# Probabilities times v: twelve rounded products on the whole array, or six float32 products on its halves

## The chip, the cores and the metric

The kernel runs on one core of a Trainium2 chip, in one launch. The core has a matrix engine (TensorE, PE in the profile; its weight loads are PEld), three engines for elementwise work (VectorE or DVE, ScalarE or ACT, GpSimd or POOL) and a queue that issues transfers (SyncE, SP). The metric is the device time of one execution in microseconds, lower is better; it is the median of several runs.

## The reference

Three layers follow one another. The first is attention for 2 batches, 8 heads, 768 positions and a head dimension of 64, in which a query sees only the keys of its own cluster:

```python
q_assign = np.argmax(np.einsum('bhsd,hcd->bhsc', q_n, c_n), axis=-1)
k_assign = np.argmax(np.einsum('bhsd,hcd->bhsc', k_n, c_n), axis=-1)
mask = q_assign[:, :, :, None] == k_assign[:, :, None, :]
scores = np.where(mask, scale * np.matmul(q, k.transpose(0, 1, 3, 2)), -1000000000.0)
attn = np.exp(scores - np.max(scores, axis=-1, keepdims=True))
attn = attn / (np.sum(attn, axis=-1, keepdims=True) + 1e-09)
out = np.matmul(attn, v)
```

The second layer takes these 1536 rows of 512 through `h = x @ w_in` (1024 wide), a softmax gate, a layer norm with gain and `@ w_out`. The third is `(x @ w_a) * (x @ w_b) @ w_out`, 1536 wide. All is float32; the weights come as 64-bit floats and are turned into float32 on the chip.

## The kernel before

**Two number formats.** Most products are made in a rounded float32 format (`F32R`, "fp32r" in the profile) in which TensorE streams one column per cycle. To keep float32's accuracy an operand is split into its rounded value (hi) and what is left (lo), and a product becomes two or three products. A plain float32 product needs no split; TensorE makes it in two passes, and each shows as an instruction of its own in the trace.

**Attention.** Sixteen heads lie in 8 pairs `n`. A step is one tile of 128 queries of one head; there are 96. Per step `score` makes four products into one of two PSUM areas (`psS0`, `psS1`), DVE takes the row maximum (L1017), ACT the exponential with the row sum (L1021). `turn` transposes the 128 x 768 probabilities in two halves of three tiles (L1045) into `psT0` and `psT1`; ACT copies each half out rounded (L1062, hi) and DVE subtracts it from PSUM (L477, lo). Two steps make a group of 256 queries, 48 in all. `apply` multiplies a group by v, in two parts (`part` 0 and 1) of three key tiles each: per key tile the stationary operand holds v's hi and lo side by side (128 columns), and hi and lo of the probabilities stream over it (L1077), six products a part, twelve a group, all into the one bank `psO`. Its lower and upper 64 rows are then added: ACT copies both halves (L1092, L1097) and POOL adds them (L1098). A last step multiplies by the inverse row sums (L1116 to L1127) and splits the result for the next layer. `do_v` makes v's hi and lo on POOL (L482, L824).

**Preparation.** q and k of the next pair are transposed, split, compared with the centroids and laid out by transfers between the steps of the present pair (L740, L838, L842, L921 on TensorE).

**The later layers.** `moe_h` (L1187), `moe_lnt` (L1260) and `moe_x2` (L1277) are the second layer; `moe2_ab` (L1330) and `moe2_y` (L1358) the third. Their weights are loaded and split by `weight` (L570 to L602) in two staging areas (`RU`).

**Order.** Nothing is issued where it is written. Every operation is added to a plan with an engine, an estimated cost, a rank and the cells of memory that it reads and writes. The planner simulates the engines with these costs, takes at each engine's free moment the ready operation with the lowest rank, and so fixes each engine's order. Ranks come from the step's number, from small tables (`SUB`, `LEAD`, `P0`, `P1`) and from a long table of corrections (`ADJ`). On the chip the engines keep that order and wait by semaphores.

**Warm-up.** `FILL` = 26 products of the identity matrix (L704 to L711) go to TensorE at the start with a rank behind all else, wherever it would have nothing to do. In the kernel before they are of four kinds: 12 transposes, 2 float32 products on the whole array (L706), 2 of 64 columns (L708), and 10 float32 products with 64 stationary columns that take the left and the right half of the array in turn (L711, `tile_position`).

Of the kernel before, what the change touches and what calls it, by code (L numbers as in the profile page):

```python
# [26 lines left out]
LO = {'lna': (12, (2, 3, 4, 5, 9, 10, 11)), 'qk0': (4, (2, 3)), 'turn': (24, ()), 'arg': (8, (2, 3, 4, 5, 6, 7)), 'w': (8, (0, 1, 2, 3, 4, 5, 6, 7)), 'xlo': (3, (0, 2)), 'vhi': (2, (0, 1)), 'rb': (3, (1, 2)), 'xhi': (3, (0, 1, 2)), 'merge': (6, (0, 1, 2, 3, 4, 5)), 'nmul': (3, (0,)), 'qk': (4, (0, 2, 3)), 'wc': (8, (0, 1, 2, 4, 5, 6, 7))}  # L27
FILL = 26

P0 = {'q': 0.676, 'a': 0.526, 's': -1.817, 'do_v': -4.684, 'do_sim0': 1.842, 'do_arg': 0.4, 'do_oh0': 7.789}  # L30
P1 = {'a': -6.508, 's': 0.229, 'do_place': 16.159, 'do_v': -8.279, 'do_sims': 3.084, 'do_arg': -13.543, 'do_oh': -1.51, 'do_ohd': -29.092, 'qk_part': -21.079}
ADJ = {
# [35 lines left out]
    "do_oh 7.0 PE": -28.061, "do_oh 7.1 ACT": -3.7, "do_oh 7.1 PE": 4.601, "do_oh ACT": -42.439,  # L68
# [157 lines left out]
    "turn ACT": -0.037, "turn DVE": -19.442,  # L226
}
BR = {'h': 3.102, 'ln': 2.949, 'lnt': 7.533, 'x2': 11.917, 'dm': 0.03, 'ts': 2.583}


class Plan:

# [158 lines left out]
def tile_cluster_attention_moe_moe2(  # L391
# [22 lines left out]
    P = 128  # L414
# [215 lines left out]
    def hlo(n):  # L630
        return X0 + 2 * 3072 if n in (1, 3) else HL_
# [810 lines left out]
```

## Time and profile before

| | |
|---|---|
| median of 3 runs | 741.63 us (741.13 to 741.98) |
| profiled execution, its own time | 741.5 us |
| its span, first to last instruction | 739.4 us |
| busy: PE, PEld | 710.1 us (96%), 620.4 us (84%) |
| busy: DVE, ACT, POOL | 455.7, 398.8, 327.7 us |
| mean granted TensorE clock | 0.986 of full |

Busy time of PE is the union of its instructions' durations, and a duration holds some 0.16 us of pipeline that overlaps the next instruction; what an instruction keeps TensorE for is therefore read from one start to the next. 2.1 us of the execution lie outside the span.

### The profile page before, as it was taken

The page shows a single profiled execution, that of the slowest core. Times are in us where ns is not written, and L with a number is a line of the kernel's source. Part 1 is how long each engine was busy: PE and PEld are TensorE (multiplying, and loading weights), DVE is VectorE, ACT ScalarE, POOL GpSimd, SP SyncE. Part 2 cuts the span into 40 slices and gives each one's busy share as a digit, 9 for nine tenths or more (in the row PEclk, how much of TensorE's full clock was granted, in tenths as well). Part 3 has the DMA queues.
Part 4 walks back from the last instruction along what each step waited for, and adds up shares of the span by engine and source line. Part 5 has one row for each costly group of instructions (what it writes and reads, how often), then busy time and mean ns, then how long its engine had stood idle before and what let it go on. Part 6 is the DMA issues. An engine that isn't in the chain of part 4 may idle for free.

```text
span 739.4 us, 11619 instructions
## 1 busy us (share of the span) xinstructions
PE 710.1 (96%) x4166; PEld 620.4 (84%) x4166; DVE 455.7 (62%) x832; ACT 398.8 (54%) x849; POOL 327.7 (44%) x405
## 2 busy tenths in 40 slices
PE   7979899899989999999999999999999999999997
PEld 5778789799879988878999989888888888888886
DVE  5867988889868988999995716863221432111123
ACT  5768789899969998566435523443122321121111
POOL 5135986668766743666542727772130600000000
PEclk9999999999989999999999999999999999999999
DMA  4266745455363410232220313332020100010011
GB/s 154 62 141 163 177 106 132 93 145 138 84 152 72 104 59 1 86 103 97 86 87 29 107 37 114 115 120 80 1 86 0 41 18 1 1 57 1 1 57 58
DMA packets 39098, 58.53 MB, mean 79 GB/s; under 512 B 3832, under 2 KB 33920, under 8 KB 39040
## 3 DMA queue, kind: packets, MB, share of 16 engines
q1 hardware_dynamic: 39040, 57.79, 27.8%
q8 instruction: 33, 0.54, 0.3%
q14 instruction: 25, 0.20, 0.1%
HBM read 36.74 MB, written 3.15 MB: 54 GB/s over the span
## 4 chain that ended last, share of the span: by engine, by line
PE 66%; DVE 10%; ACT 9%; DMA 7%; issue 4%; POOL 3%; SPq 0%; DVEq 0%; ACTq 0%; POOLq 0%
PE psS L1358 13%; PE psT L1330 13%; PE psO L1330 7%; PE psM L1330 7%; PE psS L1187 5%; DMA F<-in_moe_w_in_dram 4%; PE psO L1277 4%; PE psM L1277 3%; PE psO L1077 3%; PE psS L1013 3%; DVE R L477 3%; PE psT L1045 3%; DVE mxn L1017 3%; ACT R L1062 3%; ACT F L1021 3%
## 5 line engine op out<-in xcount | busy, mean ns | idle before, releaser
L477 DVE TENSOR_TENSOR R<-psT,R 128x384 fp32r<-128x384 f32 (+1 forms) x216 | 118.9, 565 | 29.4 <-ACT R L1062 24.4
L475 POOL TENSOR_TENSOR R<-F,R 128x512 fp32r<-128x512 f32 (+1 forms) x76 | 87.9, 1159 | 93.2 <-ACT R L601 72.4
L1344 DVE TENSOR_TENSOR R<-F,R 128x512 fp32r<-128x512 f32 x36 | 27.6, 768 | 151.5 <-ACT R L1343 151.5
L1330 PE MATMUL psT<-R 128*128 128x512 f32 x432 | 103.8, 390 | 0.2 <-ACT F L1341 0.2
L1358 PE MATMUL psS<-R 128*128 128x512 f32 x432 | 100.5, 389 | 0.0
L1045 PE MATMUL psT<-ident,F 128*128 128x128 f32 x576 | 92.1, 278 | 7.5 <-DVE R L477 6.5
L1062 ACT CAST R<-psT 128x384 fp32r<-128x384 f32 x192 | 89.6, 482 | 15.6 <-PE psT L1045 13.1
L1013 PE MATMUL psS<-R 128*128 128x512 f32 (+3 forms) x384 | 94.7, 370 | 1.0 <-ACT F L1021 0.8
L1330 PEld LDWEIGHTS psT<-R 128*128 128x128 f32 x432 | 80.8, 188 | 17.7 <-ACT F L1341 1.1
L1358 PEld LDWEIGHTS psS<-R 128*128 128x128 f32 x432 | 81.1, 188 | 16.8
L1343 ACT CAST R<-F 128x512 fp32r<-128x512 f32 x36 | 22.4, 622 | 133.5 <-PE psS L1358 132.7
L1077 PE MATMUL psO<-R 128*128 128x256 f32 x576 | 92.1, 296 | 1.9 <-ACT F L1097 1.8
L1017 DVE TENSOR_REDUCE mxn<-psS 128x1 f32<-128x768 f32 x96 | 90.7, 946 | 4.4 <-PE psS L1013 4.3
L1021 ACT ACTIVATE F<-psS,mxn 128x768 f32<-128x768 f32 x96 | 87.4, 910 | 3.3 <-DVE mxn L1017 2.9
L592 POOL TENSOR_TENSOR F<-F 128x512 int32<-128x512 int32 x45 | 61.3, 1362 | 45.7 <-DVE F L588 33.9
L1077 PEld LDWEIGHTS psO<-R 128*128 128x128 f32 x576 | 75.6, 191 | 4.4 <-ACT F L1097 3.5
L1045 PEld LDWEIGHTS psT<-ident,F 128*128 128x128 f32 x576 | 66.9, 142 | 13.8 <-DVE R L477 9.0
L1013 PEld LDWEIGHTS psS<-R 128*128 128x128 f32 (+1 forms) x384 | 68.5, 198 | 11.1 <-ACT F L1021 1.7
L1187 PE MATMUL psS<-R 128*128 128x512 f32 x288 | 69.2, 394 | 2.0 <-DVE F L1208 2.0
L570 ACT ACTIVATE F<-F 128x512 f32<-128x512 f32 x48 | 32.5, 678 | 67.8 <-DMA F<-in_moe_w_a_dram 22.3
L1187 PEld LDWEIGHTS psS<-R 128*128 128x128 f32 x288 | 52.9, 188 | 12.8 <-DVE F L1208 2.5
L1330 PE MATMUL psO<-R 128*128 128x512 f32 x216 | 51.9, 389 | 0.0
(157 smaller groups left out, 1076.8 us busy)
## 6 DMA issues: line engine op xcount, KB each, us to landing
F<-in_moe_w_out_dram SPq DMA_DIRECT2D x20, 512.0 KB, 3.2
R<-R SPq DMA_DIRECT2D x28, 288.0 KB, 5.1
F<-in_moe_w_b_dram SPq DMA_DIRECT2D x12, 512.0 KB, 3.5
F<-in_moe_w_a_dram SPq DMA_DIRECT2D x12, 512.0 KB, 3.5
R<-R SPq DMA_DIRECT2D x28, 192.0 KB, 5.3
F<-in_moe_w_in_dram SPq DMA_DIRECT2D x8, 512.0 KB, 6.0
F<-in_v_dram SPq DMA_DIRECT2D x8, 384.0 KB, 3.8
out_dram<-F SPq DMA_DIRECT2D x12, 256.0 KB, 2.1
```

Of the source, the lines that this page charges most:

```text
L475: pl.add("POOL", pool(n), rank, lambda: G.tensor_tensor(out=out_, in0=in0, in1=in1, op=ALU.subtract), reads, writes)
L477: pl.add("DVE", dve(n), rank, lambda: V.tensor_tensor(out=out_, in0=in0, in1=in1, op=ALU.subtract), reads, writes, port=port)
L592: pl.add("POOL", pool(n), rank, lambda: G.tensor_tensor(out=u, in0=u, in1=low, op=ALU.add), [rk, lwk], [uk])
L1013: T.matmul(sp[:, c0:c0 + cn], kq[:r, 2 * m, t * P:(t + 1) * P], kq[:r, 2 * m + 1, c0:c0 + cn], start=m == 0, stop=m == 1)
L1017: pl.add("DVE", dve(S), i + SUB["max"], lambda: V.tensor_reduce(out=mxn[:, b:b + 1], in_=sp[:, :S], axis=AX.X, op=ALU.max, negate=True), [ ...
L1021: pl.add("ACT", act(S) + 93 + 93, i + SUB["exp"], lambda: A.activation(F[:, po:po + 768], sp[:, :S], AF.Exp, bias=mxn[:, b:b + 1], scale=1 ...
L1045: T.transpose(sp[:, c, :], pt[:, kt * P:(kt + 1) * P], ident)
L1062: pl.add("ACT", act(HN), rk, lambda sp=sp, dh=dh: A.copy(dh, sp), [sk], [hk])
L1077: T.matmul(psO[:, :GN], vs[:, kt, j].rearrange("p l d -> p (l d)"), pt[:, m, kt, :], start=(kt == 0 and m == 0), stop=(kt == NT - 1 and m ...
L1187: T.matmul(sp[:, n0:n0 + 512], xv5[:, i, a, c], winv[:, w, c, n0:n0 + 512], start=first, stop=(c == KD - 1 and a == 1))
L1330: T.matmul(pt, w[:, l, c, :], xv5[:, xs, a, c, :], start=first, stop=(c == KD - 1 and l == 1))
L1358: T.matmul(yv[t][0], hl2[a][:, ts_], wo[:, l, :], start=(first and a == 0 and l == 0), stop=(last and a == 1))
```

## The change

A group's probabilities stay plain float32, as they come out of the transposes, and v stays as it was loaded. `apply` makes one float32 product per key tile, with the 64 columns of v as the stationary operand on one half of the array, even key tiles on the left half and odd ones on the right. A part is thus three products: left, right, left in part 0 and right, left, right in part 1. The two halves of `psO` are added as before, now by ACT (a copy) and DVE (an addition that reads PSUM). `turn` has one copy per half: `psT0` by DVE, `psT1` by ACT. `do_v` is gone, and v is loaded into one of two places of its own. All 26 warm-up products are transposes. The memory that this frees holds a fourth set of q/k operands and a second pair of split buffers (`KQS`, `HLS`), and the last layer's weight loads have four staging areas for two; three of that layer's weight pieces are loaded early for six, and 25 of them have a place for 28. The planner counts `PVC` for a part. `ADJ` has other numbers throughout, `P0` and `P1` are shorter.

```diff
+PVC = 3 * 216.0 + 15.0
+TDM, TD = 4, (0, 2)
...
-    RU = ((5376, 6400), (6912, 7936))
+    KQS, HLS = (20480, 23552, 26624, 36608), (30464, 33536)
+    VS = (1536, 6016)
+    RU = ((5376, 6400), (6912, 7936), (8448, 9472), (9984, 11008))
...
         for x in range(FILL):
-            if x < 12:
-                fn, cost = lambda: T.transpose(psO[:, :P], ident, ident), 107
-            elif x < 14:
-                fn, cost = lambda: T.matmul(psO[:, :256], ident, wide, start=True, stop=True), 107
...
+            pl.add("PE", 107, 1e6 + x, lambda: T.transpose(psO[:, :P], ident, ident), ["ident"], ["psO"])
...
-            pl.add("ACT", act(HN), rk, lambda sp=sp, dh=dh: A.copy(dh, sp), [sk], [hk])
-            sub("turn", i * 2 + hf, HN, rk, dl, sp, dh.bitcast(F32), [sk, hk], [lk])
+            if (2 * i + hf) % TDM in TD:
+                pl.add("DVE", dve(HN), rk, lambda sp=sp, dh=dh: V.tensor_copy(dh, sp), [sk], [hk])
+            else:
+                pl.add("ACT", act(HN), rk, lambda sp=sp, dh=dh: A.copy(dh, sp), [sk], [hk])
...
-                for kt in range(part * HT, (part + 1) * HT):
-                    for m in range(2):
-                        T.matmul(psO[:, :GN], vs[:, kt, j].rearrange("p l d -> p (l d)"), pt[:, m, kt, :],
-                                 start=(kt == 0 and m == 0), stop=(kt == NT - 1 and m == 1))
...
-            pl.add("PE", mm_cost(GN, 6), i + SUB["pv"] + 1 + part, mm, [rc(*rd)], ["psO"], after=70.0)
+                for kt in ks:
+                    rs = slice(kt % 2 * D, (kt % 2 + 1) * D)
+                    T.matmul(psO[rs, :GN], vs[:, j, kt % HT * 2 + kt // HT], pt[:, kt, :], start=kt < 2, stop=kt >= NT - 2,
+                             tile_position=(0, kt % 2 * D), skip_group_check=True)
...
+            pl.add("PE", PVC, i + SUB["pv"] + 1 + part, mm, [fc(*rd)], ["psO"], after=70.0)
...
-            if on_pool("merge", n * 6 + j * 3 + g):
...
-                pl.add("ACT", act(GN) + 110, rk, lambda: A.copy(tv[hi], psO[hi, :GN]), ["psO"], [tk])
-                pl.add("POOL", pool(GN), rk, lambda: G.tensor_tensor(
-                    out=xv[hi], in0=tv[hi], in1=xv[hi], op=ALU.add), [tk], [hk])
+            pl.add("DVE", dve(GN), rk, lambda: V.tensor_tensor(
+                out=xv[hi], in0=psO[hi, :GN], in1=xv[hi], op=ALU.add), ["psO"], [hk])
```

TensorE's order in the middle of the attention, before: the transposes (L1045), the scores (L1013) and, six products at a time, the parts of `apply` (L1077).

```order
L1045 MATMUL psT_67<-ident,F 128x128 x3
L1077 MATMUL psO<-R 128x256 x6
L1045 MATMUL psT_68<-ident,F 128x128 x3
L1077 MATMUL psO<-R 128x256 x6
L1045 MATMUL psT_67<-ident,F 128x128 x3
L1013 MATMUL psS_66<-R 128x512 x2
L1013 MATMUL psS_66<-R 128x256 x2
```

The same place after (L1021 transposes, L989 scores, L1047 `apply`).

```order
L1021 MATMUL psT_68<-ident,F 128x128 x3
L1047 MATMUL psO<-F 64x256 x3
L1021 MATMUL psT_67<-ident,F 128x128 x3
L989 MATMUL psS_65<-R 128x512 x2
L989 MATMUL psS_65<-R 128x256 x2
L1021 MATMUL psT_68<-ident,F 128x128 x3
L1047 MATMUL psO<-F 64x256 x3
L989 MATMUL psS_66<-R 128x512 x2
```

A part is three products for six, on 64 stationary columns, and work for the whole array stands on either side of it. Of the 96 parts 94 stand alone like this, and two stand together as six.

DVE's order there, before: two subtractions (L477) and one maximum (L1017) per step.

```order
L477 TENSOR_TENSOR R<-psT_68,R 128x3x128
L1017 TENSOR_REDUCE mxn<-psS_66 128x1
L477 TENSOR_TENSOR R<-psT_67,R 128x3x128
L1017 TENSOR_REDUCE mxn<-psS_65 128x1
L477 TENSOR_TENSOR R<-psT_68,R 128x3x128
```

After (L1028 the copy of `psT0`, L1062 the addition of the halves of `psO`, L993 the maximum).

```order
L1028 COPY F<-psT_67 128x3x128
L1062 TENSOR_TENSOR F<-psO,F 64x256
L993 TENSOR_REDUCE mxn<-psS_65 128x1
L1067 TENSOR_SCALAR rinv<-rsum 128x4
L1028 COPY F<-psT_67 128x3x128
L993 TENSOR_REDUCE mxn<-psS_66 128x1
```

One copy per step stands where there were two subtractions, and the addition is new here.

TensorE at the start, before: the warm-up products ahead of the first comparison with the centroids (L799).

```order
L774 MATMUL psT_68<-ident,F 64x128 x3
L704 MATMUL psO<-ident 128x128
L706 MATMUL psO<-ident 128x256 x2
L708 MATMUL psO<-ident 128x64 x2
L711 MATMUL psO<-ident 64x256 x10
L799 MATMUL psT_67<-cb,R 128x64 x6
```

After (L763 is L774, L702 the warm-up, L788 is L799).

```order
L763 MATMUL psT_67<-ident,F 64x128 x3
L700 MATMUL psM<-ident,F 128x128
L763 MATMUL psT_68<-ident,F 64x128 x3
L702 MATMUL psO<-ident 128x128 x13
L788 MATMUL psM<-cb,R 128x64 x6
```

Thirteen transposes stand where there were one transpose and fourteen products.

## Rows read from the trace of the kernel before

**Rows 1.** Windows: busy us (instructions) by engine, granted clock, DMA share, GB/s.
```profile
19.00:303.00 284.00, 266.09 (x1869) 241.80 (x1869) 239.44 (x437) 242.55 (x575) 176.31 (x240) 0.97 0.43 107
...
150.00:200.00 50.00, 49.14 (x368) 45.55 (x368) 45.97 (x85) 48.71 (x119) 35.66 (x49) 1.00 0.44 121
...
350.00:400.00 50.00, 50.00 (x339) 46.22 (x338) 41.81 (x96) 21.95 (x40) 19.55 (x21) 1.00 0.20 64
...
500.00:550.00 50.00, 50.00 (x223) 41.40 (x222) 13.83 (x21) 14.10 (x24) 13.72 (x13) 1.00 0.17 55
```

**Rows 2.** Timeline of PE near the attention's end: start us, us, engine line op.
```profile
285.57 0.96 PE L1013 MATMUL psS<-R 128*128 128x512 f32 x4
286.36 0.88 PE L1077 MATMUL psO<-R 128*128 128x256 f32 x6
287.08 0.82 PE L1045 MATMUL psT<-ident,F 128*128 128x128 f32 x6
287.65 3.01 PE L1187 MATMUL psS<-R 128*128 128x512 f32 x12
290.51 0.82 PE L1045 MATMUL psT<-ident,F 128*128 128x128 f32 x6
```

**Rows 3.** Groups of PE by form, 19 to 303 us: count | busy us, mean ns | idle before.
```profile
L740 PE MATMUL psM<-ident,F 128*128 128x128 f32 x81 | 15.3, 302 | 0.0
L838 PE MATMUL psM<-R,cb 128*128 128x384 f32 x56 | 13.0, 353 | 0.1
L1187 PE MATMUL psS<-R 128*128 128x512 f32 x48 | 11.8, 395 | 0.0
L1116 PE MATMUL psM<-ident,F 128*128 128x128 f32 x46 | 9.0, 276 | 0.5 <-ACT F L747 0.4
L921 PE MATMUL psM<-ident,F 128*128 128x128 f32 x42 | 7.9, 300 | 6.7 <-POOL F L893 3.5 <-ACT R L924 3.1
L842 PE MATMUL psM<-ident,F 128*128 128x128 f32 x42 | 7.3, 281 | 0.1
```

**Rows 4.** Timeline of PE in the warm-up.
```profile
7.33 0.56 PE L708 MATMUL psO<-ident 128*128 128x64 f32 x4
7.82 2.38 PE L711 MATMUL psO<-ident 128*64 128x256 f32 x20
10.12 0.41 PE L799 MATMUL psT<-cb,R 128*128 128x64 f32 x2
```

**Rows 5.** Windows of L711 alone: PE busy (instructions under way), PEld, clock, DMA.
```profile
7.80:7.83 0.03, 0.01 (x2) 0.02 (x2) 1.00 1.35 512
7.83:8.05 0.22, 0.22 (x2) 0.18 (x4) 1.00 1.01 377
8.05:8.10 0.05, 0.05 (x4) 0.02 (x2) 1.00 1.14 430
```

**Rows 6.** Chain of waits, 6.5 to 11 us: start us, us, what.
```profile
6.63 0.87 PE psO L706 x4
...
10.19 0.79 PE psT L799 x6
```

**Rows 7.** Waits of PE's weight loads, 19 to 303 us: total, times, longest.
```profile
PEld psT L1045 <- DVE R L477: 9.0, 18, 3.0
PEld psM L921 <- POOL F L893: 3.9, 2, 3.7
...
PEld psO L1077 <- ACT F L1097: 3.5, 8, 1.2
```

**Rows 8.** Groups of DVE, ACT and POOL by line, 19 to 303 us.
```profile
L477 DVE TENSOR_TENSOR R<-psT,R 128x384 fp32r<-128x384 f32 x192 | 102.7, 550 | 25.8 <-ACT R L1062 24.4
L1127 DVE TENSOR_TENSOR F<-F,psM 128x256 f32<-128x256 f32 x15 | 6.1, 408 | 0.2 <-PE psM L1116 0.2
L1062 ACT CAST R<-psT 128x384 fp32r<-128x384 f32 x192 | 89.6, 482 | 15.6 <-PE psT L1045 13.1
L1097 ACT COPY F<-psO 64x256 f32<-64x256 f32 x47 | 17.2, 367 | 0.6
```

More of the change, by code (lines that the diff above doesn't have):

```diff
@@ L441, in tile_cluster_attention_moe_moe2 @@
     ps = ctx.enter_context(tc.tile_pool(name="ps", bufs=1, space=PSUM))
[L444 to L447 removed]
+    X0, WIN_, OHT_ = 0, 12288, 29696
+    KQS, HLS = (20480, 23552, 26624, 36608), (30464, 33536)
+    WO_, EW_, LNT_, HLC_ = 20480, 28672, 31744, 12288 + 6144
+    R = const.tile([P, 39936], F32R, name="R")
+    NAT_, P_, SIM_, OHP_, XS_, RB_, PT_ = 0, 2304, 3840, 4224, 4992, 5760, 8448
+    VS = (1536, 6016)
     E_, LN_, WG_, ACC_, BS_ = 0, 2048, 4096, 0, 4096
[L449 to L452 removed]
+    RU = ((5376, 6400), (6912, 7936), (8448, 9472), (9984, 11008))
+    OUT_, CT_ = 5376, 11520
+    F = const.tile([P, 11904], F32, name="F")
     psS = [ps.tile([P, 1024], F32, name=f"psS{i}") for i in range(2)]
@@ L609, in tile_cluster_attention_moe_moe2 @@
     NPR = len(pairs)
-    nat = [F[:, NAT_ + 768 * i:NAT_ + 768 * (i + 1)].rearrange("p (h t d) -> p h t d", h=2, t=NT) for i in range(3)]
+    nat = [F[:, NAT_ + 768 * i:NAT_ + 768 * (i + 1)].rearrange("p (h t d) -> p h t d", h=2, t=NT) for i in range(2)]
     nat1 = [F[:, RU[1][0] + 768 * i:RU[1][0] + 768 * (i + 1)].rearrange("p (h t d) -> p h t d", h=2, t=NT) for i in range(2)]
@@ L630, in hlo @@
     def hlo(n):
-        return X0 + 2 * 3072 if n in (1, 3) else HL_
+        return HLS[n % 2]
     def hlv(n):
@@ L700, in centroids @@
         pl.add("PE", 213, Rk, lambda: T.transpose(psM[:, :P], F[:, CT_ + 128:CT_ + 256], ident), [cd, "ident"], ["psM"])
-        wide = ident.unsqueeze(1).to_broadcast([P, 2, P])
         for x in range(FILL):
-            if x < 12:
-                fn, cost = lambda: T.transpose(psO[:, :P], ident, ident), 107
-            elif x < 14:
-                fn, cost = lambda: T.matmul(psO[:, :256], ident, wide, start=True, stop=True), 107
-            elif x < 16:
-                fn, cost = lambda: T.matmul(psO[:, :D], ident, ident[:, :D], start=True, stop=True), 107
-            else:
-                rs = slice(x % 2 * D, (x % 2 + 1) * D)
-                fn, cost = lambda rs=rs: T.matmul(psO[rs, :256], ident[:, :D], wide, start=True, stop=True,
-                                                  tile_position=(0, rs.start), skip_group_check=True), 107
-            pl.add("PE", cost, 1e6 + x, fn, ["ident"], ["psO"])
+            pl.add("PE", 107, 1e6 + x, lambda: T.transpose(psO[:, :P], ident, ident), ["ident"], ["psO"])
         cpv = psM[:, :P].rearrange("p (a h c) -> p a h c", a=NHP, h=2)
@@ L816, in do_place @@
             dma((0, 96 * (d1 - d0)) if rows else (96 * (d1 - d0), 0), rk, lambda dst=dst, src=src: Y.dma_start(dst.bitcast(F32), src.bitcast(F32)), rd, wr)
-    def do_v(n, j, rk):
-        vs = vsv(n).rearrange("p (r a) j l d -> p r a j l d", r=2)
-        vh, vl = vs[:, :, :, j, j, :], vs[:, :, :, j, 1 - j, :]
-        src = nat[2][:, j].rearrange("p (a r) d -> p r a d", r=2)
-        ck = rc(*[(vso(n) + t * 256 + j * 128, 128) for t in range(NT)])
-        copy("vhi", n * 2 + j, 384, rk, vh, src, [natk(n, 2)], [ck])
-        pl.add("POOL", pool(384), rk, lambda: G.tensor_tensor(
-            out=vl, in0=src, in1=vh.bitcast(F32), op=ALU.subtract), [natk(n, 2)], [ck])
     def do_sims(n, s, rk, bk):
@@ L1045, in tr @@
                     T.transpose(sp[:, c, :], pt[:, kt * P:(kt + 1) * P], ident)
-            dh = dst[:, 0, hf * HT:(hf + 1) * HT, tt * P:(tt + 1) * P]
-            dl = dst[:, 1, hf * HT:(hf + 1) * HT, tt * P:(tt + 1) * P]
-            hk, lk = (rc(*[(o + m * 1536 + kt * 256 + tt * P, P) for kt in range(hf * HT, (hf + 1) * HT)]) for m in range(2))
+            dh = dst[:, hf * HT:(hf + 1) * HT, tt * P:(tt + 1) * P]
+            hk = fc(*[(o + kt * 256 + tt * P, P) for kt in range(hf * HT, (hf + 1) * HT)])
             rk = i + SUB["t1" if hf else "t0"]
             pl.add("PE", 330, rk, tr, [pk], [sk])
-            if on_pool("turn", i * 2 + hf):
-                so = OHT_ + 768 + hf * HN
-                st = R[:, so:so + HN].bitcast(F32).rearrange("p (c n) -> p c n", c=HT)
-                tk = rc((so, HN))
-                pl.add("ACT", act(HN), rk, lambda sp=sp, st=st: A.copy(st, sp), [sk], [tk])
-                pl.add("POOL", 150 + 0.86 * HN, rk, lambda st=st, dh=dh: G.tensor_scalar(
-                    out=dh, in0=st, scalar1=1.0, scalar2=0.0, op0=ALU.mult, op1=ALU.add), [tk], [hk])
-                pl.add("POOL", pool(HN), rk, lambda st=st, dh=dh, dl=dl: G.tensor_tensor(
-                    out=dl, in0=st, in1=dh.bitcast(F32), op=ALU.subtract), [tk, hk], [lk])
-                continue
-            pl.add("ACT", act(HN), rk, lambda sp=sp, dh=dh: A.copy(dh, sp), [sk], [hk])
-            sub("turn", i * 2 + hf, HN, rk, dl, sp, dh.bitcast(F32), [sk, hk], [lk])
+            if (2 * i + hf) % TDM in TD:
+                pl.add("DVE", dve(HN), rk, lambda sp=sp, dh=dh: V.tensor_copy(dh, sp), [sk], [hk])
+            else:
+                pl.add("ACT", act(HN), rk, lambda sp=sp, dh=dh: A.copy(dh, sp), [sk], [hk])
     def apply(i, part):
@@ L1092, in apply @@
             pl.add("ACT", act(GN) + 110, rk, lambda: A.copy(xv[hi], psO[lo, :GN]), ["psO"], [hk])
-            if on_pool("merge", n * 6 + j * 3 + g):
-                to = XT_ + g % 2 * 256
-                tv = F[:, to:to + 256]
-                tk = fc((to, 256), rows=1 << j)
-                pl.add("ACT", act(GN) + 110, rk, lambda: A.copy(tv[hi], psO[hi, :GN]), ["psO"], [tk])
-                pl.add("POOL", pool(GN), rk, lambda: G.tensor_tensor(
-                    out=xv[hi], in0=tv[hi], in1=xv[hi], op=ALU.add), [tk], [hk])
-            else:
-                pl.add("DVE", dve(GN), rk, lambda: V.tensor_tensor(
-                    out=xv[hi], in0=psO[hi, :GN], in1=xv[hi], op=ALU.add), ["psO"], [hk])
+            pl.add("DVE", dve(GN), rk, lambda: V.tensor_tensor(
+                out=xv[hi], in0=psO[hi, :GN], in1=xv[hi], op=ALU.add), ["psO"], [hk])
             return
@@ L1118, in apply @@
         pl.add("PE", 2 * 107, rk, tr, [rbk], ["psM"])
-        if on_pool("nmul", n * 3 + g):
-            to = XN_ + g % 2 * 256
-            tv = F[:, to:to + 256]
-            tk = fc((to, 256))
-            pl.add("ACT", act(GN), rk, lambda: A.copy(tv, psM[:, :GN]), ["psM"], [tk])
-            pl.add("POOL", pool(GN), rk, lambda: G.tensor_tensor(
-                out=xv, in0=xv, in1=tv, op=ALU.mult), [tk], [xk])
-        else:
-            pl.add("DVE", dve(GN), rk, lambda: V.tensor_tensor(
-                out=xv, in0=xv, in1=psM[:, :GN], op=ALU.mult), ["psM"], [xk])
+        pl.add("DVE", dve(GN), rk, lambda: V.tensor_tensor(
+            out=xv, in0=xv, in1=psM[:, :GN], op=ALU.mult), ["psM"], [xk])
         ts = range(b * NT + g * GT, b * NT + (g + 1) * GT)
@@ L1292, in tile_cluster_attention_moe_moe2 @@
     US = 3.27
-    PIECES = [EW_ + i * 1024 for i in range(6)] + [WIN_ + i * 1024 for i in range(6)]
+    PIECES = [EW_ + i * 1024 for i in range(3)] + [WIN_ + i * 1024 for i in range(6)]
     PIECES += [LNT_ + i * 1024 for i in range(8)] + [WO_ + i * 1024 for i in range(8)]
@@ L1311, in load_w2 @@
         o = piece(f, x)
-        weight(rank, src, shp, o, o + 512, RU[(f * 3 + x) % 2], "ACT", f * 3 + x)
+        weight(rank, src, shp, o, o + 512, RU[(f * 3 + x) % 4], "ACT", f * 3 + x)
     outv = out.rearrange("(b p a r) d -> b r a p d", b=B, a=HT, r=2)
```

201 lines of the change are left out of this document (92 added, 109 removed), and 232 rows, old and new, of the table ADJ.

## The prediction

> **What bounds the kernel now.** I read the windows first. From 350 us to the end TensorE is busy all the time (50.00 of 50 us) while the others fall to a third of that [rows 1]: the two later layers are bound by TensorE, the change leaves their products as they are, and what the attention gains or loses arrives at the end undiminished. The attention, 19 to 303 us, is different: PE 266, ACT 243, DVE 239 of 284 us, and in its best stretch (150 to 200 us) PE 49.1 and ACT 48.7 of 50 [rows 1]. Three engines are near their limit, and PE first.
>
> A busy PE is no measure, so I counted what the work keeps TensorE for, start to start. In the timeline the four score products of a step take 285.57 to 286.36 = 0.79 us, one part of `apply` 0.72, the six transposes 0.57: 2.08 per step, 200 us for 96 steps [rows 2]. The groups by form add 211 transposes (81 + 46 + 42 + 42) at 0.11 (the six with the tail that the next product's start hides), 23 us, and 56 products of 384 columns at 0.18 (by columns from the 0.12 of a product of 256), 10 us, and 48 of the second layer at 2.86 / 12, 11 us [rows 2, 3]; some 2 us are small. That is **246 us of work in 284**, so 38 us are lost: 17.9 visibly idle (284.0 - 266.1), about 8 by the clock (0.97 granted on the mean, 284 x 0.03), the rest in gaps that lie under the pipeline's overlap [rows 1]. The waits of the weight loads name the causes: 9.0 us for DVE's subtraction that frees `psT`, 3.5 for ACT's second copy that frees `psO`, and 3.9 for the cluster masks of the next pair [rows 7].
>
> **What leaves ACT, DVE and POOL.** DVE loses 192 subtractions of 0.550 and gets 96 copies of 384 elements from PSUM; the trace has no such copy in bulk, so between 0.482 (ACT's copy of the same tile) and 0.550, and I take 0.55. It also gets 48 additions at about 0.41 (the like one of L1127): 103 - 53 - 20 = 30 us less, 209 of 284. ACT loses 96 copies of 0.482 and 48 of 0.367, 64 us, and stands at 179 [rows 8]. POOL loses the additions and v's split. None of these three can bound the attention any more, and the waits for `psT`'s subtraction and for the second copy of `psO` have nothing left to wait for but one copy or one addition.
>
> **What the new product costs TensorE.** This is the term that decides, and the warm-up of before happens to contain it: L711 is the float32 product with 64 stationary and 256 streamed columns, left and right half in turn. Ten products are 20 instructions, two passes each [rows 4]. Two weight loads start at once and two more some 0.05 later, two passes start together, and the next two only after 8.05 [rows 5]; ten pairs lie between 7.82 and 10.12 [rows 4]. A whole-array float32 product has two passes of 0.87 / 4 = 0.217 [rows 6], and ten times that is 2.17. So a pass on a half takes as long as one on the whole array; what the halves save is that a left and a right pass run side by side.
>
> In the warm-up that is ten products in ten slots. A part of `apply` is **three** products, left, right, left, and work for the whole array stands on both sides. The left half has two products, four passes, one after another; the right half's two passes run beside the first two and it is then empty. That is four slots, 4 x 0.217 = 0.87 us, not three. To it comes the way into the half mode and out of it: L711 keeps TensorE 2.30 where its slots make 2.17, so 0.13 more (the first weight load, which nothing hides, and the wait before L799), and L708's four passes take 0.49, where four passes of 64 columns made one after another for L799 take 4 x 0.79 / 6 = 0.53 [rows 4, 6] or, by their columns, 0.22; the entry thus costs between nothing and 0.27, and I take 0.10. **A lone part costs 0.87 + 0.23 = 1.10 us, where six rounded products cost 0.72: 0.38 more.** Its bounds: 0.15 more if entry and exit are hidden, 0.55 more with the dear entry, and 0.07 less if three products took three slots (0.65) and the switches nothing. 94 lone parts at 0.38 and the one pair (six slots and one switch, 1.53 against 1.44) make **+36 us of TensorE's work**, 282 in place of 246.
>
> The Trainium skill (TensorEngine Tiling, Theoretical Speedup) has an array split in two for 64 columns or fewer at up to twice the speed. By it a part would be 3 x 0.435 / 2 = 0.65 and the change would save TensorE 7 us. The trace bears that out for an even, unbroken alternation only.
>
> **What of the 38 lost us goes.** With 282 us of work TensorE is the one bound, and the pace of a step stays near the old 2.96 us (284 / 96) while DVE has an eighth and ACT a quarter less to do. I take away the waits for `psT` and `psO` (9.0 + 3.5, and 1.5 of like ones), 4 of the 6.7 us before the masks' transposes, since POOL has less in its queue [rows 3, 7], and 5 of the 8 at the slow clock, since fewer long waits let it fall: 23. That leaves 15, between 0 and the whole 38. Those who wait behind DVE's new copy and addition are its maximum (L1017 before) and through it the exponential; with DVE at 209 of 284 I cost that at nothing, and it would cost part of the 38 if the cover were gone.
>
> **The rest.** The warm-up before L799 shrinks from 7.33 to 10.12 to transposes of 0.11, thirteen in all: at most 1.4 us earlier, and I take 1. v's loads go straight to their place, one transfer per pair as before, so SP's queue has the same number. The fourth set of q/k operands lets the placing transfers start earlier; nothing waits for them in the weight loads' list. The last layer has fewer weight pieces early and more staging areas; TensorE does not wait from 350 us on [rows 1], the three other engines that split the weights have spare time there, and if that cover were too thin a piece's load and split would show as a gap of some us. All that at nothing, ± 2.
>
> **The sum**, against the profiled execution's 741.5 (0.1 below the median of 741.63): + 36 - 23 - 1 = + 12, **753.5, forecast 753**.
>
> **The rivals.**
> *The switches hide (faster).* The next weights are loaded during the lone left passes, and the last whole-array product drains beside the first half products; or the second passes pair better and a part takes three slots plus the switches (0.65 + 0.23). Then a part costs 0.87 to 0.88, 0.15 more, 14 us; - 23 - 1 makes **731**. For it: weight loads run ahead of products all through the trace. Against it: the one stretch of half products in the trace holds TensorE 0.13 longer than its slots [rows 4, 6], and in it nothing of L799 ran ahead. With neither extra slot nor switch it would be 720. The point from which it decides: a part under 0.97 us (24 / 95 + 0.72). Chance 0.20.
> The skill (TensorEngine Tiling, Key Properties) says that a change of tiling mode drains TensorE; this speaks against hidden switches, it names no price, and the two switches of rows 4 agree with it.
> *TensorE fills completely.* All 38 us go: + 36 - 38 - 1 = **738 to 742**, no change. For it: from 350 us on it does run without a gap. Against it: the first head's chain, in which nothing else is ready, and the masks' transposes wait for other engines' results and not for a free one. Chance 0.08.
> *The waits stay (slower still).* Other orders, one `psO` whose addition now stands in DVE's queue, and a clock that falls more often because a lone half counts for little: nothing of the 38 goes, 741.5 + 36 - 1 = **776**. For it: the granted clock is 0.97 on the attention's mean already [rows 1]. Against it: rows 7 names waits that the change removes. Chance 0.10.
> *The forecast*, 743 to 764: chance 0.62.
>
> **How the numbers follow.** What can be told from no change is 0.2%, 1.5 us. Faster: 0.20 of the first rival, 0.04 of the second (its 738 to 740) and 0.03 of the forecast's lower tail, 0.27. Same: the rest of the second and 0.01 of that tail, 0.05. Slower: 0.58 of the forecast and 0.10 of the third, 0.68. The range takes in the first rival's middle and most of the third: 729 to 774; the forecast's own is 743 to 764.
>
> **What would show it.** In the profile after, a part of `apply` keeps TensorE 1.10 us to the next operation's start, and its six passes start as two pairs and then two alone; if it is under 0.97, the first rival holds. PE's busy time in the attention is over 96%, ACT and DVE stand at some 60 and 70%, and the attention ends about 12 us later. From 350 us on nothing may differ but the shift. I am wrong if a part costs 1.1 and the end is still not later: then the 38 us were worth more than I gave back.

## The result, and the profile after

The changed kernel takes **751.48 us** (median of 4 runs, 750.52 to 752.12) where the kernel before took 741.69 in the same comparison (741.13 to 741.98): a ratio of 1.0132, 95% interval 1.0114 to 1.0149. It is slower by 9.8 us; 12 had been forecast. The profiled executions have spans of 739.4 and 750.3 us.

The windows of the changed kernel, in the columns and stretches of [rows 1]:

```profile
19.00:303.00 284.00, 279.02 (x1793) 201.26 (x1792) 206.48 (x375) 186.10 (x413) 112.28 (x150) 0.99 0.42 106
150.00:200.00 50.00, 50.00 (x329) 35.84 (x327) 35.62 (x66) 34.33 (x77) 20.98 (x28) 1.00 0.40 101
350.00:400.00 50.00, 49.32 (x334) 45.44 (x332) 45.46 (x101) 23.44 (x43) 28.05 (x28) 1.00 0.28 91
500.00:550.00 50.00, 50.00 (x223) 41.40 (x222) 13.19 (x18) 12.76 (x23) 8.83 (x10) 1.00 0.13 43
```

In the attention TensorE is busy for 279 of 284 us (266 before), DVE for 206 (239), ACT for 186 (243), POOL for 112 (176). Three engines were near their limit; now one is, and it shows no idle time between 150 and 200 us.

TensorE's timeline near the attention's end, which answers to [rows 2]:

```profile
284.64 1.08 PE L1047 MATMUL psO<-F 128*64 128x256 f32 x6
285.65 0.88 PE L1021 MATMUL psT<-ident,F 128*128 128x128 f32 x6
286.28 0.96 PE L989 MATMUL psS<-R 128*128 128x512 f32 x4
287.17 1.08 PE L1047 MATMUL psO<-F 128*64 128x256 f32 x6
```

From start to start, a part of `apply` keeps TensorE 1.01 us (0.72 before), the six transposes behind it 0.63 (0.57), and the four scores ahead of it, whose end holds the change into the half mode, 0.89 (0.79). A step is 2.53 us where it was 2.08: 0.45 more, though the part has half as many products.

Most parts stand behind transposes and not behind scores. The first two rows are such a part after, the last two one before:

```profile
115.64 0.82 PE L1021 MATMUL psT<-ident,F 128*128 128x128 f32 x6
116.39 1.08 PE L1047 MATMUL psO<-F 128*64 128x256 f32 x6
```
```profile
284.52 0.96 PE L1077 MATMUL psO<-R 128*128 128x256 f32 x6
285.32 0.49 PE L1045 MATMUL psT<-ident,F 128*128 128x128 f32 x3
```

Six transposes ahead of a part keep TensorE 0.75 us (0.57 elsewhere), so the way into the half mode takes 0.18 there. But a rounded part behind transposes kept it 0.80 and not 0.72, so the change again costs 0.45: 0.18 ahead, 0.21 in the part (1.01 for 0.80) and 0.06 behind.

The windows of L1047 alone over one part (PE busy with the instructions under way, PEld, clock, DMA) answer to [rows 5]:

```profile
201.48:201.70 0.22, 0.21 (x2) 0.20 (x4) 1.00 0.32 105
201.70:201.75 0.05, 0.05 (x2) 0.00 (x0) 1.00 0.09 31
201.75:201.96 0.21, 0.21 (x4) 0.14 (x1) 1.00 0.16 37
201.96:202.18 0.22, 0.22 (x3) 0.14 (x1) 1.00 0.12 35
202.18:202.49 0.31, 0.31 (x2) 0.00 (x0) 1.00 0.09 30
```

Two passes start in the first window, two in the third, and one each in the fourth and the fifth (the counts hold passes that are still ending): two pairs and then two alone, four slots, as forecast.

Groups of DVE and ACT by line, 19 to 303 us, against [rows 8]:

```profile
L1028 DVE COPY F<-psT 128x384 f32<-128x384 f32 x94 | 52.0, 553 | 34.5 <-PE psT L1021 30.7 <-PE psO L1047 3.4
L1062 DVE TENSOR_TENSOR F<-psO,F 64x256 f32<-64x256 f32 x46 | 19.2, 418 | 7.5 <-ACT F L1061 6.8
```
```profile
L1030 ACT COPY F<-psT 128x384 f32<-128x384 f32 x94 | 45.0, 478 | 29.0 <-PE psT L1021 27.4
L1061 ACT COPY F<-psO 64x256 f32<-64x256 f32 x46 | 16.8, 366 | 26.2 <-PE psO L1047 25.5 <-POOL F L870 0.4
```

The new copy is 0.553 us and the new addition 0.418 (0.55 and 0.41 were taken). What ends most of the idle time of the copies is TensorE; the addition mostly waits for ACT's copy of the other half (6.8 of 7.5 us).

The waits of PE's weight loads that named other engines, 19 to 303 us, against [rows 7]:

```profile
PEld psT L1021 <- ACT F L997: 3.3, 8, 0.7
PEld psT L1021 <- ACT F L1030: 3.0, 8, 0.4
PEld psO L1047 <- DVE F L1062: 2.2, 5, 1.5
```

The largest was 9.0; the subtraction and the masks are gone from the list, and the addition in DVE's queue that one rival feared is worth 2.2.

Where the attention begins and ends: the first row is the first score product after; the next two are the last part of `apply` and what follows it, after; the last three are the same of before.

```profile
15.63 1.63 PE L989 MATMUL psS<-R 128*128 128x512 f32 x4
...
315.25 1.08 PE L1047 MATMUL psO<-F 128*64 128x256 f32 x6
316.26 11.18 PE L1140 MATMUL psS<-R 128*128 128x512 f32 x48
```
```profile
18.43 1.83 PE L1013 MATMUL psS<-R 128*128 128x512 f32 x3
...
302.42 0.88 PE L1077 MATMUL psO<-R 128*128 128x256 f32 x6
303.13 0.38 PE L1116 MATMUL psM<-ident,F 128*128 128x128 f32 x2
```

So the attention lasts 300.6 us for 284.7 (+15.9), begins 2.8 earlier, and what follows it takes 434.0 (750.3 - 316.3) for 436.3 (-2.2): +10.9 of span.

### The profile page after: what moved, and what is told of

Same layout as the page of the kernel before. It is cut to its first block, busy times and chain, and to the rows that moved or that the text cites. A ratio compares the mean times of both kernels' runs of the same rounds, so it can differ in the third digit from the quotient of the medians.

```text
span 750.3 us, 11135 instructions
## 1 busy us (share of the span) xinstructions
PE 735.9 (98%) x4152; PEld 590.3 (79%) x4152; DVE 444.6 (59%) x792; ACT 348.6 (46%) x697; POOL 269.4 (36%) x317
## 4 chain that ended last, share of the span: by engine, by line
PE 89%; DVE 5%; DMA 2%; ACT 1%; POOL 1%; issue 1%; SPq 0%; DVEq 0%; ACTq 0%; POOLq 0%
PE psS L1311 13%; PE psT L1283 13%; PE psO L1047 13%; PE psT L1021 9%; PE psS L989 9%; PE psO L1283 7%; PE psM L1283 7%; PE psS L1140 5%; PE psO L1230 4%; PE psM L1230 4%; PE psM L729 1%; PE psM L818 1%; DMA F<-in_moe_w_in_dram 1%; PE psT L1213 1%; DMA F<-in_moe_w_out_dram 1%; PE psM L901 1%
## 5 line engine op out<-in xcount | busy, mean ns | idle before, releaser
L1047 PE MATMUL psO<-F 128*64 128x256 f32 x576 | 104.2, 400 | 1.3 <-DVE F L1062 1.3
L1311 PE MATMUL psS<-R 128*128 128x512 f32 x432 | 103.5, 389 | 0.0
L993 DVE TENSOR_REDUCE mxn<-psS 128x1 f32<-128x768 f32 x96 | 91.3, 952 | 17.8 <-PE psS L989 16.2
L989 PE MATMUL psS<-R 128*128 128x512 f32 (+3 forms) x384 | 92.9, 365 | 0.0
L1021 PE MATMUL psT<-ident,F 128*128 128x128 f32 x576 | 90.4, 278 | 0.9 <-ACT F L997 0.4
L1021 PEld LDWEIGHTS psT<-ident,F 128*128 128x128 f32 x576 | 64.8, 140 | 22.7 <-issue 9.2
L989 PEld LDWEIGHTS psS<-R 128*128 128x128 f32 (+1 forms) x384 | 66.5, 193 | 14.5 <-issue 4.6
L1028 DVE COPY F<-psT 128x384 f32<-128x384 f32 x96 | 53.1, 553 | 34.7 <-PE psT L1021 30.9
L1047 PEld LDWEIGHTS psO<-F 128*64 128x64 f32 x576 | 45.7, 137 | 32.9 <-issue 13.4
L1140 PE MATMUL psS<-R 128*128 128x512 f32 x288 | 69.7, 395 | 0.7 <-DVE F L1161 0.7
L1294 ACT COPY F<-psT 128x512 f32<-128x512 f32 x36 | 21.1, 586 | 97.3 <-PE psT L1283 95.7
L1030 ACT COPY F<-psT 128x384 f32<-128x384 f32 x96 | 45.9, 478 | 34.5 <-PE psT L1021 32.9
L1295 DVE TENSOR_TENSOR F<-psO,F 128x512 f32<-128x512 f32 x18 | 12.4, 691 | 73.5 <-PE psO L1283 73.5
L1295 DVE TENSOR_TENSOR F<-psM,F 128x512 f32<-128x512 f32 x18 | 12.4, 690 | 72.5 <-PE psM L1283 72.5
```

The costliest lines, as they stand in the source:

```text
L989: T.matmul(sp[:, c0:c0 + cn], kq[:r, 2 * m, t * P:(t + 1) * P], kq[:r, 2 * m + 1, c0:c0 + cn], start=m == 0, stop=m == 1)
L993: pl.add("DVE", dve(S), i + SUB["max"], lambda: V.tensor_reduce(out=mxn[:, b:b + 1], in_=sp[:, :S], axis=AX.X, op=ALU.max, negate=True), [ ...
L1021: T.transpose(sp[:, c, :], pt[:, kt * P:(kt + 1) * P], ident)
L1028: pl.add("DVE", dve(HN), rk, lambda sp=sp, dh=dh: V.tensor_copy(dh, sp), [sk], [hk])
L1047: T.matmul(psO[rs, :GN], vs[:, j, kt % HT * 2 + kt // HT], pt[:, kt, :], start=kt < 2, stop=kt >= NT - 2, tile_position=(0, kt % 2 * D), s ...
L1140: T.matmul(sp[:, n0:n0 + 512], xv5[:, i, a, c], winv[:, w, c, n0:n0 + 512], start=first, stop=(c == KD - 1 and a == 1))
```

## The experiments

Theory: TensorE is the bound of the changed attention, and a lone part costs it four slots and two changes of mode. Rivals: the part is long by its changes of mode alone; the time is lost in new waits; the other engines' relief decides. Each run is timed beside the kernel before, whose median was 739.95 to 740.86 us in these comparisons.

### A fourth product in a part: g3

```diff
-            ks = range(part * HT, (part + 1) * HT)
+            ks = (3, 4, 5, 4) if part else (0, 1, 2, 1)
...
```

The flags that open and close the sums follow the new sequence; each engine's order is that of the changed kernel.

> The changed kernel in its own order, each part with a fourth half product (key tile 1 again behind 0, 1, 2; key tile 4 again behind 3, 4, 5): a second pair in place of a product that runs alone, 96 products more, two key tiles count twice in the output. Theory (a lone part of three takes four slots of 0.217 us because the other half of the array stands empty beside its third product): the fourth product fits into the empty slots, 751 us, range 749 to 754. Rival (a product costs its own time, the part is long because of the two switches alone): 96 products of 0.22 to 0.31 us, 772 to 781. Second rival (TensorE was not the bound): 751 as well, but then the busy share of TensorE in the attention is not 98%.

Measured: 753.48 us (752.12 to 754.00), ratio 1.016 [1.0127, 1.0193]. TensorE's timeline in this kernel:

```profile
283.93 1.08 PE L1047 MATMUL psO<-F 128*64 128x256 f32 x8
284.94 0.87 PE L1021 MATMUL psT<-ident,F 128*128 128x128 f32 x6
285.57 0.94 PE L989 MATMUL psS<-R 128*128 128x512 f32 x4
286.44 1.08 PE L1047 MATMUL psO<-F 128*64 128x256 f32 x8
287.46 0.87 PE L1021 MATMUL psT<-ident,F 128*128 128x128 f32 x6
```

A part with four products (eight instructions) keeps TensorE 1.01 us, to the hundredth what three keep it. 96 products more cost 2 us together, which the two intervals don't tell from nothing (1.0127 to 1.0193 here, 1.0114 to 1.0149 for the changed kernel), and TensorE is as busy as in the changed kernel (279.04 of 284 us), so the second rival falls too. This is the clearest evidence for the four slots: the right half stood empty.

### Parts of two and four, each engine's order kept: f2

The order that the planner made for the changed kernel stays as it is; only what a part issues differs.

```diff
-            ks = range(part * HT, (part + 1) * HT)
+            ks = range(2, NT) if part else range(2)
```

A product of part 1 then reads a key tile that some groups' next but one group has already rewritten; the output of those groups is not the reference's.

> As e2 (parts of two and four), in the changed kernel's own order. Theory: two slots a group fewer, 21 us of TensorE's work, some 3 to 6 given back: 733 to 739; f1 lies below it by the price of 48 switches, 14 us, or what the waits leave of it. Rival (switches alone cost, an empty half does not): 749 to 753.

Measured: 734.45 us (734.11 to 734.95), ratio 0.9911 [0.9896, 0.9926]: 17 us under the changed kernel by the same products, from 2 slots per group fewer (0.43 x 48 = 21 us of TensorE). The rival of 749 to 753 falls.

### Products on halves in the kernel before: f4

The orders, copies, subtractions and merges of before, with the three half products on the rounded parts for the six products; the lower parts of the probabilities and of v are made and left out.

```diff
-                    for m in range(2):
-                        T.matmul(psO[:, :GN], vs[:, kt, j].rearrange("p l d -> p (l d)"), pt[:, m, kt, :],
-                                 start=(kt == 0 and m == 0), stop=(kt == NT - 1 and m == 1))
+                    rs = slice(kt % 2 * D, (kt % 2 + 1) * D)
+                    T.matmul(psO[rs, :GN], vs[:, kt, j, j].bitcast(F32), pt[:, 0, kt, :].bitcast(F32), start=kt < 2, stop=kt >= NT - 2,
+                             tile_position=(0, kt % 2 * D), skip_group_check=True)
```

> The kernel before, all as it is (splits, subtractions, additions on POOL, order), with the changed kernel's six half products a group on the rounded hi parts for its twelve; the lo parts are left out of the result. It has the change's cost on TensorE without its relief. Theory: 95 parts at 0.44 us more (1.16 by the changed kernel's trace, 0.72 before) are 42 us of work on top of 246 in an attention of 284, of which at most the present waits, up to 38 us, absorb some: 755 to 775, above the changed kernel's 751. Rival (the change's relief is worth nothing, TensorE's work alone sets the end): 749 to 753.

Measured: 759.85 us (758.76 to 760.64), ratio 1.0252 [1.0235, 1.027]. The first row is its window of the attention, the others its timeline: a part in the middle, and the attention's end (it begins at 18.78 us).

```profile
19.00:303.00 284.00, 277.32 (x1782) 197.94 (x1782) 229.86 (x416) 236.43 (x558) 166.99 (x229) 1.00 0.43 106
```
```profile
285.60 1.08 PE L1077 MATMUL psO<-R 128*64 128x256 f32 x6
286.61 0.88 PE L1045 MATMUL psT<-ident,F 128*128 128x128 f32 x6
...
319.68 1.08 PE L1077 MATMUL psO<-R 128*64 128x256 f32 x6
320.69 0.44 PE L1116 MATMUL psM<-ident,F 128*128 128x128 f32 x2
```

The part is 1.01 us here too. The attention lasts 301.9 us, 17.2 more than before. The products add about 42 us of work (96 x 0.44), so 25 us of the lost time filled **with DVE, ACT and POOL still carrying what they carried**. Of these, 11 are visible idle time (17.9 before, 6.7 here) and about 8 the clock (0.97 and 1.00 granted on the mean, 284 x 0.03); the rest lay in gaps under the pipeline's overlap. The changed kernel, with their relief and its own order, has 300.6: within the attention both together bring 1.3 us. The two spans (756.7 and 750.3 us) differ by 6.4; the other 5.1 lie outside, 3.1 in the start and 2.0 in what follows.

### Relief without the new product: f3

The kernel before, its order kept, without the 192 subtractions; the rounded probabilities are streamed twice, and their lower parts are left out.

```diff
-            sub("turn", i * 2 + hf, HN, rk, dl, sp, dh.bitcast(F32), [sk, hk], [lk])
+            pl.add("DVE", dve(HN), rk, lambda: None, [sk, hk], [lk])
...
-                        T.matmul(psO[:, :GN], vs[:, kt, j].rearrange("p l d -> p (l d)"), pt[:, m, kt, :],
+                        T.matmul(psO[:, :GN], vs[:, kt, j].rearrange("p l d -> p (l d)"), pt[:, 0, kt, :],
```

> As e3 (the kernel before without the subtraction, hi streamed twice, the probabilities' lo part left out), with the order of the kernel before in every engine, the subtractions' places empty. Theory (a third to a half of the 38 us lost in the attention before are waits that a less busy DVE takes away): 724 to 733. Rival (they do not depend on DVE's load): 739 to 743.

Measured: 735.39 us (734.58 to 738.11), ratio 0.993 [0.9907, 0.9952]: 5.4 us for taking away all of DVE's subtractions, between the two expectations. The window shows DVE down from 239 to 161 us and ACT's 247 as high as before:

```profile
19.00:303.00 284.00, 269.48 (x1908) 245.47 (x1907) 161.20 (x259) 246.66 (x585) 182.52 (x247) 0.98 0.44 112
```

TensorE gains 3.4 us of busy time in it. The waits of its weight loads for DVE's subtraction are gone from the list, and those for ACT have grown (3.5 and 1.7 us before):

```profile
PEld psO L1077 <- ACT F L1097: 4.9, 14, 1.2
PEld psS L1013 <- ACT F L1021: 4.2, 8, 1.6
```

So with the wait that named DVE for 9.0 us gone, 5.4 us of time came back; I take it that ACT, which comes next behind DVE, holds the rest. No run relieves ACT or POOL by itself.

### The planner's count of a part: e4

The changed kernel, whose planner counts 1.10 us for a part in place of 0.66; only the orders differ.

```diff
-PVC = 3 * 216.0 + 15.0
+PVC = 1100.0
```

> The changed kernel with the planner told 1.10 us for a part in place of 0.66. Nothing else differs but the order. Theory (TensorE is busy without a gap from 100 to 300 us, so the order of the rest hardly matters): 749 to 753. Rival (the plan's wrong cost is what made the change slow): under 745.

Measured: 789.94 us (789.11 to 792.34), ratio 1.066 [1.0618, 1.0703], a miss by 37 us. The window of 150 to 200 us and the first two waits of PE, 19 to 313 us, in this kernel:

```profile
150.00:200.00 50.00, 38.80 (x224) 27.47 (x223) 29.04 (x54) 22.54 (x51) 23.37 (x34) 0.88 0.44 106
```
```profile
PE psM L1077 <- POOL F L486: 7.8, 2, 4.0
PE psT L1021 <- ACT F L997: 5.8, 4, 3.1
```

TensorE, busy for all of the 50 us in the changed kernel, stands still for 11 of them, with a granted clock of 0.88 there. Each engine issues the same operations as in the changed kernel, in another order, so order alone is worth 38 us here. Why this order is so much worse is read from the code and not shown: `ADJ` holds offsets that fit one plan; with another duration the planner makes other orders, and the offsets then put work in the wrong place.

### Variants that the planner ordered anew: e1, e2, e3

All six products in one run (e1), parts of two and four with their own reads (e2), and the kernel before without subtractions, whose lower parts are left out (e3), each planned anew.

```diff
+            if part == 0:
+                return
+            ks = range(NT)
...
+            pl.add("PE", 2 * PVC, i + SUB["pv"] + 1 + part, mm, [fc(*rd)], ["psO"], after=70.0)
```

> The changed kernel with a group's six half products in one run, left and right in turn, where they were two lone runs of three. Theory (four slots a part and a switch into and out of the half mode bound it, and TensorE is the limit): a lone part kept TensorE 1.16 us in the changed kernel's trace; six in a row take six slots and one switch, 0.09 + 0.27 + 5 x 0.216 + 0.15 = 1.59 us, 0.73 less per group, 35 us for 48 groups. Some of the waits come back as TensorE has less to do: 716 to 732, about 724. Rival (the attention now waits for the one bank psO and for DVE's addition, or for other engines, not for TensorE's own time): 742 to 752, no better than the kernel before.

> The changed kernel with parts of two and four products (left, right / left, right, left, right) for three and three: as many runs and switches as before this edit, but no slot with an empty half. Theory: two slots per group are saved, 2 x 0.216 x 48 = 21 us of TensorE's work, about 15 to 20 of them in the time: 731 to 738. What lies between this and the run of six is the price of a switch, 48 of them, 0.29 us each by the trace. Rival (passes pair up without regard to halves, three products take three slots and only the switches cost): no change, 749 to 753.

> The kernel before, with the probabilities' lo part left out of the result: the subtraction on DVE is not made and the hi part is streamed twice, so that TensorE has the same twelve products a group and DVE 103 us less. Theory (38 us of the attention were lost to waits, a third of it for the subtraction that frees psT, and the change took back 23 to 26 of them by relieving the other engines): 741.7 less 9 to 18, 724 to 733. Rival (the lost time lies in latencies that do not depend on how busy the other engines are): 739 to 743.

Measured: e1 765.49 us, ratio 1.0321 [1.0276, 1.0366]; e2 771.67, 1.0427 [1.0374, 1.048]; e3 756.18, 1.0203 [1.016, 1.0247]. All three miss by 23 us or more on the slow side. After e4 they prove nothing of the products or of the subtractions: e2 and f2 issue the same ones, and e2 is 37 us slower by its order. That is why the other runs keep the orders.

### Six in one run, orders kept: f1 and g2

```diff
-            ks = range(part * HT, (part + 1) * HT)
+            ks = range(NT) if part else ()
```

In f1 some groups meet a later group's probabilities, as in f2.

> As e1 (six half products in one run), but planned with the changed kernel's costs and parts, so that every engine's order is the changed kernel's own; the first part's place is empty and the second's holds all six. Theory (TensorE's time in lone parts of four slots and two switches a group is what the change costs): 35 us less work for TensorE, 12 to 15 of them given back as waits: 725 to 737, about 729. Rival (the new order with its waits on psO and DVE bounds the attention, as e1's result could also be read): 745 to 760.

Measured: 737.83 us (735.49 to 739.93), ratio 0.9967 [0.9944, 0.9989], 0.8 over the range's upper end and 3 slower than f2. The groups of PE, 19 to 303 us, in this kernel:

```profile
L1021 PE MATMUL psT<-ident,F 128*128 128x128 f32 x576 | 90.7, 278 | 4.9 <-ACT F L1030 2.1 <-ACT F L997 1.3 <-DVE F L1028 0.4
...
L729 PE MATMUL psM<-ident,F 128*128 128x128 f32 x81 | 14.0, 282 | 4.2 <-DVE F L1080 2.5 <-ACT F L736 1.1 <-ACT R L904 0.2
```

It has 48 runs of half products fewer than f2, some 14 us of work, and its transposes wait again. g2 is f1 with three places for the first half of the probabilities. The third place overlaps memory that the second pair's operands and the last weights use, so its output is not the reference's either.

> The kernel with all six products in one run, in the changed kernel's order, first halves in three places. By TensorE's slots alone (one run per group fewer, 48 pairs of switches at 0.27 to 0.29 us = 13 to 14 us under the parts of two and four) 720 us; by the waits that came back in the earlier run of six products (psT copies of ACT, DVE's copies late) 736 to 740. The second is expected: 738, range 735 to 741.

Measured: 738.55 us (735.75 to 741.73), ratio 0.9964 [0.9937, 0.999]: the same, so late reads are not what holds f1 back.

### Parts of two and four with places of their own: g1 and g4

g1 gives f2 the third place of g2, with the same overlap.

> The kernel with parts of two and four products in the changed kernel's order, the probabilities' first halves rotating over three places, so that a late read finds its own group. Theory (TensorE's slots decide: six slots per group in place of eight, no price for the third place): 734 us, range 732 to 738, faster than both kernels. Rival (the earlier time came from data that was read while it was rewritten, or the third place collides with transfers): 739 to 750.

Measured: 735.76 us (734.22 to 738.09), ratio 0.9927 [0.9903, 0.9951]. g4 computes all of the reference: the first halves and second halves of each group have places chosen by a table in one more column of 256, so that no read comes after a later write; the orders are those of the changed kernel on every engine.

```diff
-    F = const.tile([P, 11904], F32, name="F")
+    F = const.tile([P, 12160], F32, name="F")
...
+    AT = {0: (1, 1, 4, 1), 1: (7, 1, 10, 1), 8: (2, -1, 3, 1), 9: (7, 1, 11, 1), 10: (2, 4, 1, 2), 11: (8, -4, 11, 1),
+          12: (1, 1, 5, 1), 13: (8, 1, 11, 1), 36: (2, -1, 3, 1), 37: (7, 1, 11, 1), 38: (2, 4, 3, 1), 39: (7, 1, 11, 1)}
+    def place(n, j, g, hf):
+        q = n * 6 + j * 3 + g
+        a, s = AT.get(q, (q % 2 * 6, 1, q % 2 * 6 + 3, 1))[2 * hf:2 * hf + 2]
```

> The parts of two and four products in the changed kernel's order, the probabilities' places chosen group by group in 14 columns of tiles so that no late read meets a later group's data and no late weight transfer meets a read. Theory (six slots of TensorE per group in place of eight, the place costs nothing): 734.5 us, range 732 to 737, faster than the kernel before by 0.5 to 1.2% and than the changed one by 2.0 to 2.5%. Rival (a strided place costs ACT and DVE time in their copies, or the gain came from reads that didn't wait for their own group): 740 to 751.

Measured: **734.65 us** (733.97 to 737.00), ratio 0.9932 [0.9907, 0.9957] against the kernel before: faster than both. Its timeline (L1057 is `apply`, L1031 the transposes, L1150 the products of the second layer):

```profile
280.61 1.08 PE L1057 MATMUL psO<-F 128*64 128x256 f32 x8
281.63 0.55 PE L1031 MATMUL psT<-ident,F 128*128 128x128 f32 x3
...
285.91 0.65 PE L1057 MATMUL psO<-F 128*64 128x256 f32 x4
286.50 3.02 PE L1150 MATMUL psS<-R 128*128 128x512 f32 x12
...
298.86 1.08 PE L1057 MATMUL psO<-F 128*64 128x256 f32 x8
299.88 11.19 PE L1150 MATMUL psS<-R 128*128 128x512 f32 x48
```

The part of two is 0.59 us, the part of four 1.02: 1.61 per group where the changed kernel has 2.02, and the attention ends 16.4 us earlier than there.

## Why the prediction was right, point by point

- **What bounds the kernel.** Right. After the change TensorE is the one bound of the attention (279 of 284 us), f2 and g4 get back 17 us by its slots alone, and 96 products in empty slots cost 2 us (g3). From 350 us on the kernel differs by little more than its shift (49.3 and 50.0 of 50 us busy).
- **The part of `apply`.** Right in kind and a little small. 0.87 for the slots, 0.13 at the exit and 0.10 at the entry were forecast, 1.10. Measured are 1.01 from its first start to the next operation's, and 0.10 more in the scores ahead. Left out were 0.06 in the transposes behind: a step is 0.45 longer, of which I count 0.44 as the part's, for the forecast 0.38. Over the 94 lone parts and the pair that is some 42 us for 36. The Trainium skill (TensorEngine Tiling, Key Properties) says that a change of mode drains TensorE; the trace is in line with it, with some 0.3 us for the way in and out behind scores (1.01 + 0.10 + 0.06 - 0.87) and 0.38 behind transposes (0.18 in place of 0.10).
- **The rival of hidden switches** wanted a part under 0.97 us, and falls by the same rows; its 720 without slot and switch does not follow from the prediction's own terms (741.5 - 7 - 24 is 710). The Trainium skill (TensorEngine Tiling, Theoretical Speedup) has up to twice the speed with 64 columns. The 0.65 us that was worked out from it for a part falls too, the rule does not: a part of three has 4 slots of the 6 that the array unsplit would take, and a part of four has 4 of 8, the full factor of two, before the switches.
- **What of the lost time goes.** 23 of 38 us were given back; it was about 26: the attention lengthened by 15.9 for 42 us of work. The size is near and its reason mostly wrong. The prediction let the waits go because DVE, ACT and POOL were relieved. f4 relieves none of them, and 25 us fill all the same. I read that so: TensorE spends longer between two requests, and more of the others' results are there in time. The relief alone, of DVE, is worth 5.4 us where TensorE has slack (f3). The term for the clock held: 5 of its 8 us were to come back, and 0.99 was granted for 0.97.
- **The 38 us themselves** were too many. The prediction took 0.72 us for every part of before, from one that stands behind scores; 80 of the 96 stand behind transposes, where a part keeps TensorE 0.80. By my estimate that is 6 us more work (80 x 0.08), 252, and some 32 us lost.
- **The rival in which the waits stay** (776) falls by the 279 us and the waits list; that in which TensorE fills completely (738 to 742) falls too: 12.6 us stay lost by the prediction's 246 (300.6 - 246 - 42), some 7 by 252. It came closer than the prediction thought: TensorE is idle for 5.0 of 284 us only.
- **The start and the rest.** 1 us was taken for the warm-up, and the attention begins 2.8 us earlier. The shorter warm-up is one cause; this start was planned anew as well, and no run splits the two. The rest was costed at nothing, ± 2, and is 2.2 shorter. The groups from the attention's end (303 and 316 us) to 520 us, before and after, show 1.3 of that as a wait of the second layer for DVE:

```profile
L1187 PE MATMUL psS<-R 128*128 128x512 f32 x240 | 57.4, 393 | 2.0 <-DVE F L1208 2.0
```
```profile
L1140 PE MATMUL psS<-R 128*128 128x512 f32 x240 | 57.7, 394 | 0.7 <-DVE F L1161 0.7
```

- **The sum with measured terms**: + 42 - 26 - 2.8 - 2.2 = + 11 us of span, for + 36 - 23 - 1 = + 12. A part too small by 6 and three gains too small by 7 together cancelled: that the sum came so near is luck.
- **The order** stands in the prediction only as one ground of the rival in which the waits stay, and no term of the sum is for it. e4 shows that another order of the same work moves the time by 38 us, more than any term of the sum. The forecast took the order as one that keeps the pace, and it did.

**Open.** Why six products in one run are not faster than two and four: f1 has less work for TensorE than f2 and 7.7 us more idle time (busy 269.0 and 276.7 us of 284), in waits for results of ACT and DVE. Whether an order planned for it would take that away wasn't tried: the offsets would have to be made anew.

## What to carry to other kernels

Count products on half arrays in slots, not in products: an odd run leaves a half of the array empty for one product, and each run pays the way in and out, so group them in even numbers and as few runs as the waits bear (g4: 734.65 us with 2 and 4, 751.48 with 3 and 3). When the bounding engine gets more work, part of it can go into idle time between its requests, even if no other engine is relieved: here 25 of 42 us. Where an order was fitted to one set of costs, test a change with the order held fixed, or the order's own 38 us will be read as the change's.

## What the runs showed of the hardware

- A float32 product on one half of the array takes as long as on the whole one (passes 0.22 us apart for 256 columns; [rows 6] has 0.217 on the whole array), and a product on the other half beside it costs nothing: 1.01 us for three products, 1.01 for four.
- The way into the half mode and out of it costs about 0.3 us per run behind rounded products, spread over three operations (0.10 ahead, 0.14 within, 0.06 behind), and nearer 0.4 behind transposes (0.18 ahead), so a run's own row shows less than half of it.
- A run of rounded products behind float32 transposes keeps TensorE longer than behind rounded ones: 0.80 and 0.72 us for the six products of a part before.
- In f4 the granted clock is 1.00 on the attention's mean (0.97 before), though half products stand in it for the rounded ones of the whole array. From 200 to 250 us, before and in f4:

```profile
200.00:250.00 50.00, 46.16 (x322) 42.54 (x321) 38.90 (x71) 40.66 (x98) 35.13 (x50) 0.93 0.54 129
```
```profile
200.00:250.00 50.00, 48.45 (x316) 34.80 (x315) 39.82 (x70) 41.90 (x100) 33.39 (x46) 1.00 0.43 105
```

In this stretch before, TensorE waits 3.5 us for the masks and the clock falls to its lower level for a time (0.93 on the mean); in f4 it is busier and the clock stays at the upper one. The prediction's rival in which half products make the clock fall more often is not borne out.
